# Sigmoid attention and two token-mixing layers on one core: pairs of token batches alternate in short runs of blocks, and attention takes its own order of work

## The chip, the cores and the metric

The kernel runs on one core of a Trainium2 chip. The metric is device time in microseconds (us) of the whole program. TensorE (PE) multiplies, VectorE (DVE), ScalarE (ACT) and GpSimd (POOL) work on the tiles in on-chip memory, and SyncE (SP) issues most DMA transfers. Each of these engines takes its instructions strictly in the order in which they were written.

## The reference, cut to what matters

```python
def _attn_ref(q, k, v):                       # q, k, v: (4, 12, 448, 64), float32
    scale = 1.0 / np.sqrt(q.shape[-1])
    scores = scale * np.matmul(q, k.transpose(0, 1, 3, 2)) - np.log(q.shape[2])
    return np.matmul(1.0 / (1.0 + np.exp(-scores)), v)
def _moe_ref(x, w_in, w_out):                 # x: (1792, 768), 2048 hidden columns
    h = x @ w_in
    return (h - np.tanh(h)) @ w_out
def _moe2_ref(x, w_gate, w_val, w_out):       # 1536 hidden columns
    gate = 1.0 / (1.0 + np.exp(-(x @ w_gate)))
    return (gate * (x @ w_val)) @ w_out
def reference(**kwargs):
    ...
    x = attn_out.transpose(0, 2, 1, 3).reshape(B * S, H * D)
    x = _moe_ref(x=x, **moe_kwargs)
    return _moe2_ref(x=x, **moe2_kwargs)
```

All is float32. The kernel holds each float32 operand as a high and a low part (fp32r) and makes one product of it out of three matmuls.

## The kernel before

**Attention** comes first: 24 pairs of heads, written by the loop at the end of the program. For a pair, `scores` (L1561 to L1597) multiplies keys and queries: PE fills the banks `sl` (L1573) and `sa` (L1588), and ACT takes the sigmoid out of them into `al` (L1577) and `at` (L1592, three a pair). `split` (L1525) is DVE's part: it divides keys and queries of the next pair into `sp` (seven instructions, L1538 to L1547), from which PE makes `sa`. `values` (L1616) multiplies the pair before with its values, and ACT copies the result into `x` (L1632). When the last pair of heads of a batch is done, `x` of that batch goes to DRAM as `xs` (L1634, 1,344 KB).

**The two layers** are worked through in 28 blocks of hidden columns for a pair of the four token batches. A block's hidden part is seven products of quarter tiles (`product`, L1996, 63 matmuls for each hidden matrix), over the terms a11, s1, s2, a12, s3, s4, a22 of x, some of them sums of quarters of x. `prepare` (L1415) makes these terms: the sums at L1435, the high part on ACT at L1443, the low parts on DVE or POOL at L1457. The projection of a block (`plain`, L1687, 72 matmuls; or `wide_fillers`, L1809, 63 matmuls) is worked into the hidden part of the block after it; the last one is `last_projections` (L1873). A block of layer 1 has 135 matmuls with a plain projection, one of layer 2 198, or 189 with a wide one.

**The passes.** The blocks run in four passes: layer 1 for the first pair of batches (8 blocks), layer 1 for the second (8), layer 2 for the first (6), layer 2 for the second (6). In the first pass of a layer the weights come from the inputs as raw words of 64 bits (`raw_task`, L1015, tiles `st`) and are decoded (`decode`, L1030): the absolute value on ACT (L1048), a clamp on DVE or POOL (L1054), and three more steps on DVE (L1061, L1067, L1073). The decoded words `mw` or `ms` are divided into high and low parts (`divide_for`, L1158: high on ACT L1186, low on DVE or POOL L1195, sums of quarters L1226, L1239), and the halves are stored in DRAM (L1206). In the second pass of the layer `bring` (L1261) loads the halves back (L1282) and nothing is decoded. Seven weights of layer 2 are decoded ahead, in the second pass of layer 1, and kept in DRAM as words (`MID`).

**The order** is written out by hand under `manual_schedule`. A planner in the program writes it: work other than matmuls is a `Task` (L860) with a due time and a list of operations, each with a planned cost on one or two engines, and `spend` (L932) lets the tasks onto the engines beside a stretch of matmuls, by due time. The times at which blocks and passes begin, the offsets of the due times and the choice of engines come from a table of numbers, `TUNE`. In the attention `tick` gives tasks half a pair's time, twice a pair:

```python
scores(p)
tick()
split(p + 1)
if p:
    load_v(p + 2)
    values(p - 1)
tick()
```

Names in the rows: `pa`, `pb`, `pc`, `pe` are PSUM banks of the hidden part, `pq` those of the projection, `sg` what the activation is taken of, `gg` its result divided again, `y` the sum over the blocks (L1673).

## Time and profile before

| | us |
|---|---|
| median of 3 runs | 1116.19 |
| the runs | 1116.50, 1116.19, 1112.31 |
| the profiled execution, its own time | 1112.16 |
| its span | 1110.4 |

| engine | busy in the span |
|---|---|
| PE (matmuls) | 1055.8 us, 95% |
| DVE | 872.5 us, 79% |
| ACT | 631.4 us, 57% |
| POOL | 286.6 us, 26% |

The rows further down come from the profiled execution, so sums are made against its 1112.16 us, of which 1.76 lie outside the span. PE is the engine with the most work; the time that it isn't at work at full pace can be read as losses: in a stretch with n matmuls of the layers, the stretch's length minus n times the length of one in an undisturbed stretch. The granted clock of PE is given for each window as a share of full speed.

### The profile page before, as it was taken

How to read it: one execution, taken by the hardware profiler on the slowest of the kernel's cores; microseconds unless marked ns; L12 is line 12 of the kernel's file. 1: busy time of each engine (PE TensorE's matmuls, PEld its weight loads, DVE VectorE, ACT ScalarE, POOL GpSimd, SP SyncE). 2: the span in 40 equal slices, each digit the busy share in tenths (PEclk: the TensorE clock that was granted, in tenths of full speed). 3: DMA queues.
4: the chain of work that ended last, by engine and by line, in shares of the span. 5: the costliest groups of instructions: out<-in, count | busy, mean ns of one | idle time of the engine just before them, and what ended most of it. 6: DMA issues, size and time to landing. Idle time of an engine off the chain costs nothing.

```text
span 1110.4 us, 16236 instructions
## 1 busy us (share of the span) xinstructions
PE 1055.8 (95%) x5895; PEld 943.3 (85%) x5895; DVE 872.5 (79%) x1432; ACT 631.4 (57%) x1038; POOL 286.6 (26%) x269
## 2 busy tenths in 40 slices
...
GB/s 214 235 287 214 266 117 341 181 182 176 208 185 183 216 213 213 213 199 228 213 214 99 185 341 214 199 203 296 219 320 218 272 206 138 165 182 189 173 9 102
...
## 3 DMA queue, kind: packets, MB, share of 16 engines
...
q10 hardware_dynamic: 160, 0.23, 0.1%
...
## 4 chain that ended last, share of the span: by engine, by line
PE 73%; DVE 12%; ACT 6%; DMA 3%; issue 3%; SPq 2%; POOL 1%; ACTq 0%; POOLq 0%; DVEq 0%
PE pq L1724 24%; PE pa L1996 11%; PE pb L1996 11%; PE pc L1996 11%; PE pe L1996 6%; PE pv L1626 3%; PE pq_c L1785 1%; DVE y L1673 1%; SPq L1504 1%; PE sa L1588 1%; PE pq_a L1785 1%; PE pq_b L1785 1%; DVE mw L1067 1%; PE sl L1573 1%; DVE mw L1073 1%
## 5 line engine op out<-in xcount | busy, mean ns | idle before, releaser
L1724 PE MATMUL pq<-gg,w 128*128 128x448 f32 x1656 | 357.9, 366 | 15.4 <-ACT y L1733 10.0
L1724 PEld LDWEIGHTS pq<-gg,w 128*128 128x128 f32 x1656 | 312.6, 189 | 41.5 <-ACT y L1733 11.5
L1996 PE MATMUL pa<-a,w_b 128*128 128x448 f32 x720 | 159.1, 365 | 4.7 <-DVE sg L2059 4.7
L1996 PEld LDWEIGHTS pa<-a,w_b 128*128 128x128 f32 x720 | 135.9, 189 | 14.9 <-DVE sg L2059 5.4
L1673 DVE TENSOR_TENSOR y<-pq,y 128x448 f32<-128x448 f32 x171 | 105.3, 619 | 27.5 <-PE pq L1724 26.8
L1195 POOL TENSOR_TENSOR w<-mw,w 128x384 fp32r<-128x384 f32 x29 | 33.8, 1170 | 215.8 <-ACT w L1186 160.5
L1996 PE MATMUL pb<-s,w_t 128*128 128x448 f32 x360 | 79.2, 363 | 2.6 <-ACT pb L2015 1.5
L1996 PE MATMUL pe<-s,w_t 128*128 128x448 f32 x360 | 79.3, 364 | 1.5 <-DVE sg L2059 1.1
L1996 PE MATMUL pb<-s,w_b 128*128 128x448 f32 x360 | 79.4, 364 | 1.0 <-DVE s L1457 1.0
L1996 PE MATMUL pc<-a,w_t 128*128 128x448 f32 x360 | 79.2, 363 | 1.0 <-DVE a L1457 0.6
L1996 PE MATMUL pc<-s,w_t 128*128 128x448 f32 x360 | 78.5, 362 | 0.0
L1996 PEld LDWEIGHTS pb<-s,w_t 128*128 128x128 f32 x360 | 67.1, 187 | 8.7 <-ACT pb L2015 2.3
L1996 PEld LDWEIGHTS pe<-s,w_t 128*128 128x128 f32 x360 | 67.9, 189 | 6.9 <-DVE sg L2059 1.5
L1996 PEld LDWEIGHTS pb<-s,w_b 128*128 128x128 f32 x360 | 68.2, 189 | 6.0 <-DVE s L1457 1.4
L1996 PEld LDWEIGHTS pc<-a,w_t 128*128 128x128 f32 x360 | 67.4, 187 | 6.5 <-DVE a L1457 1.3
L1996 PEld LDWEIGHTS pc<-s,w_t 128*128 128x128 f32 x360 | 67.5, 187 | 4.5
L1592 ACT ACTIVATE at<-sa,bias_s 128x896 f32<-128x896 f32 x72 | 67.1, 1008 | 5.4 <-PE sa L1588 5.4
L1626 PE MATMUL pv<-at,vt 128*64 128x224 f32 x576 | 63.5, 373 | 0.0
L1195 POOL TENSOR_TENSOR w_b<-mw,w_b 128x384 fp32r<-128x384 f32 x18 | 21.7, 1208 | 152.0 <-ACT w_b L1186 120.5
L1195 DVE TENSOR_TENSOR w_t<-mw,w_t 128x384 fp32r<-128x384 f32 x84 | 50.2, 633 | 11.6 <-ACT w_t L1186 11.3
L1626 PEld LDWEIGHTS pv<-at,vt 128*64 128x64 f32 x576 | 41.2, 143 | 20.9 <-issue 8.3
L1186 ACT ACTIVATE w_t<-mw 128x768 fp32r<-128x768 f32 x50 | 41.3, 841 | 29.3 <-DVE mw L1226 17.6
...
## 6 DMA issues: line engine op xcount, KB each, us to landing
...
```

Of the source, the lines that this page charges most:

```text
L1067: nc.vector.scalar_tensor_tensor(out=mine(), in0=t_[0][0][:, :, 1], scalar=-0x40000000, in1=mine(), op0=ALU.bitwise_and, op1=ALU.bitwise_or,)
L1073: nc.vector.scalar_tensor_tensor(out=mine(), in0=t_[0][0][:, :, 0], scalar=29, in1=mine(), op0=ALU.logical_shift_right, op1=ALU.bitwise_or,)
L1186: nc.scalar.activation(out=w0, in_=src, func=AF.Copy)
L1195: eng.tensor_tensor(out=w1, in0=quarter(m, qs[i]), in1=w0.bitcast(F32), op=ALU.subtract)
L1504: by.dma_start(out=t[r], in_=src[p, r, j])
L1573: nc.tensor.matmul(pl[h * KL:(h + 1) * KL, j, :SH], kt[r, KR:], qt[r, h * SH:(h + 1) * SH], start=True, stop=True,)
L1592: nc.scalar.activation(out=at[:, :, c], in_=pa[:, :, :S], func=AF.Sigmoid, bias=bias_s, scale=qk_scale,)
L1626: nc.tensor.matmul(po[j * D:(j + 1) * D, h, :SH], vt[:, j, c], at[:, j, c, h * SH:(h + 1) * SH], start=False, stop=(c == NCH - 2),)
L1673: nc.vector.tensor_tensor(out=at[:, d], in0=po, in1=at[:, d], op=ALU.add)
L1724: nc.tensor.matmul(po[:, :S], wk[use, j][:, a, d], gt[t][:, c, j], start=i == 0 and not seeded, stop=i == 5, skip_group_check=seeded,)
L1785: nc.tensor.matmul(o, w[:, a, h * KH + d], move[x](b), start=fresh and i == 0, stop=i == 2, skip_group_check=not fresh,)
L1996: nc.tensor.matmul(bank[term], w[:, i, half * KH + c], t[:, j, c], start=fresh and at == 0, stop=at == 3 * KH - 1, skip_group_check=not fresh,
```

## The change

The pairs of batches now alternate every 4 blocks in layer 1 and every 3 in layer 2 (`ORDER`): blocks 0 to 3 first pair, 4 to 11 second pair, 12 to 15 first pair; in layer 2 blocks 16 to 18 second pair, 19 to 24 first, 25 to 27 second. So blocks 0 to 3, 8 to 11, 16 to 18 and 22 to 24 decode their weights, and the others bring halves back. When a pair returns (block 12, block 25), the terms of x that were made for it the first time are loaded from DRAM (`again`), where `save` has put them: 14 transfers of 1,376 KB out and 14 back. Weights are decoded ahead and kept as words in three stretches in which halves are brought back: 1, 3 and 3 of them. The wide projections are those of blocks 25 to 27; before they were those of 22 to 25 and 27. The program has 18 matmuls more by this.

In the attention the loop gives tasks a whole pair's time once, after `scores` and `split`; the absolute value and the high parts may be taken by DVE there; the first conversions of x come in three pieces of 448 columns; raw words are asked for by the planned time of their first use; and `x` of batches 2 and 3 is stored after block 0. The clamp no longer goes to POOL. In the last projection three additions go to POOL by way of a copy. The count of misfits (a check at the change of layers) is a task, with its verdict two blocks later. `TUNE` has 1,145 entries instead of 711; its rows are left out here.

```diff
-TUNE = {'ahead': 117.79,
+TUNE = {'ahead': 88.65,
...
-    FIRST = [0, NF[0], 2 * NF[0], 2 * NF[0] + NF[1]]
-    NK = 2 * (NF[0] + NF[1])
-    PASS = [p for p in range(4) for _ in range(NF[p // 2])]
-    F_OF = [k - FIRST[PASS[k]] for k in range(NK)]
-    N1 = FIRST[2]
-    LAST = [len(PARTS[p // 2]) - 1 for p in PASS]
-    WIDE = TUNE.get("wide", [*range(FIRST[1], FIRST[2]), *range(FIRST[3], NK)])
+    ORDER = TUNE.get("order", (
+        (0, 0, 0, 4), (0, 1, 0, 4), (0, 1, 4, 8), (0, 0, 4, 8),
+        (1, 1, 0, 3), (1, 0, 0, 3), (1, 0, 3, 6), (1, 1, 3, 6),
+    ))
+    BLOCKS = [(l, p, f, n) for n, (l, p, f0, f1) in enumerate(ORDER) for f in range(f0, f1)]
+    NK = len(BLOCKS)
+    LAYER, PAIR, F_OF, SEG = ([b[i] for b in BLOCKS] for i in range(4))
+    DEC = [
+        not any(BLOCKS[j][0] == l and BLOCKS[j][2] == f for j in range(k))
+        for k, (l, p, f, n) in enumerate(BLOCKS)
+    ]
+    XS = [0]
+    for k_ in range(1, NK):
+        XS.append(XS[-1] + (BLOCKS[k_][:2] != BLOCKS[k_ - 1][:2]))
+    NSET = XS[-1] + 1
+    START = [XS.index(n) for n in range(NSET)]
+    STOPS = [*(n - 1 for n in START[1:]), NK - 1]
+    SET_OF = [(LAYER[n], PAIR[n]) for n in START]
+    SEG_AT = [SEG.index(n) for n in range(len(ORDER))] + [NK]
+    N1 = LAYER.index(1)
+    LAST = [len(PARTS[l]) - 1 for l in LAYER]
+    WIDE = TUNE.get("wide", range(START[-1], NK))
...
+        def plan(self):
+
+            n = len(self.ops)
+            d = [1e9] * n
+            for i in reversed(range(n)):
+                if self.by[i] is not None:
+                    d[i] = min(d[i], self.due + self.by[i])
+                if i < n - 1:
+                    d[i] = min(d[i], d[i + 1])
+                kinds, _, after, _, _ = self.ops[i]
+                before = d[i] - RF * min(kinds.values()) - RC
+                for j in after:
+                    d[j] = min(d[j], before)
+            self.dues = d
+            self.due = d[0]
...
-        def a():
+        def a(e="a"):
             t_.append(raw_t[key])
             t = t_[0][0]
+            if e == "v":
+                x = t[:, :, 1].bitcast(F32)
+                nc.vector.scalar_tensor_tensor(
+                    out=mine().bitcast(F32), in0=x, scalar=-1.0, in1=x, op0=ALU.mult, op1=ALU.max
+                )
+                return
...
-        def clamp(eng):
+        def clamp():
             m_ = mine()
-            eng.tensor_scalar(
+            nc.vector.tensor_scalar(
...
-        t = task.add(dict(a=0.78), a, (), gate)
-        t = task.add(dict(v=0.52, g=TUNE.get("pc", 1.9)), clamp, [t], lock=True)
+        t = task.add(dict(a=0.78, v=0.93) if now[0] < 0 else dict(a=0.78), a, (), gate, False)
+        t = task.add(dict(v=0.52), clamp, [t], lock=True)
...
-            for h in range(2):
-                raw_task(layer, part, 2 * f + h, due - TUNE.get("raw", 14.0) + 4.0 * h)
+        raws = [raw_task(layer, part, 2 * f + h, 0.0) for h in range(2)] if direct else ()
...
+        for raw, first in zip(raws, firsts if direct else ()):
+            raw.due = task.dues[first] - TUNE.get("raw", 5.0) + TUNE.get(raw.name, 0.0)
...
+            cost = dict(a=0.41, v=0.3) if small else dict(a=0.75, v=0.5)
+            if now[0] >= 0:
+                del cost["v"]
+            h = task.add(cost, high, after, gate, False)
...
-    ][:TUNE.get("early", 4)]
-    MID = [wid_of(u) for u in uses if PASS[u[0]] == 2][:TUNE.get("mid", 8)]
+        wid_of(u) for u in uses if SEG[u[0]] == 0 and u not in FIRST_USES
+    ][:TUNE.get("early", 2)]
+    MID = {}
+    for n_ in range(2, len(ORDER)):
+        if DEC[SEG_AT[n_]]:
+            a_, b_ = T[SEG_AT[n_ - 1]], T[SEG_AT[n_]]
+            mids = [wid_of(u) for u in uses if SEG[u[0]] == n_][:TUNE.get(f"mid{n_}", 4)]
+            for i, w in enumerate(mids):
+                MID[w] = a_ + (b_ - a_) * (i + 1) / (len(mids) + 0.5)
...
-        side = 0
+        side = early_side() if now[0] < 0 else 0
...
-        direct = PASS[k] % 2 == 0 and wid not in EARLY and wid not in MID
+        direct = DEC[k] and wid not in EARLY and wid not in MID
...
+            pieces = KH if p == 0 else 1
...
+        if SET_OF[p] in SET_OF[p + 1:]:
+            for term in TERMS:
+                save(p, term, conv[term])
+
+    def save(p, term, task):
+
+        keep = saves[p, term] = Task(
+            f"v{term}_{p}", T[START[p]] + 30.0 + 8.0 * TERMS.index(term), [task]
+        )
+
+        def f():
+            xk[p, term] = keep_p.tile([128, 2, KH, S], F32, tag=f"xk{term}{p}", name=f"xk{term}{p}_")
+            nc.sync.dma_start(out=xk[p, term], in_=xo[p, term].bitcast(F32))
+            xk_at[p, term] = keep.end[-1] + 1.0
+
+        keep.add(dict(s=1376.0), f, (), lambda: None if now[0] < 20.0 else BEGIN)
+
+    def again(p, first, due, pitch):
+        def one(term, due):
+            task = x_task[p, term] = Task(f"x{term}_{p}", due)
+
+            def gate():
+                free, got = x_free.get((p, term)), xk_at.get((first, term))
+                return None if free is None or got is None else max(free, got)
+
+            def load():
+                xo[p, term] = x_tile(PLACE[p][term], f"{term}_{p}")
+                nc.sync.dma_start(out=xo[p, term].bitcast(F32), in_=xk[first, term])
+
+            task.add(dict(s=1376.0), load, (), gate)
+
+        for i, term in enumerate(TERMS):
+            one(term, due + pitch * i)
...
-        if hp == KD - 1:
+        if hp == KD - 1 and b < 2:
...
+        copies = acc["temps"][:, KH:]
+        added = {}
+
         def p5(d, place):
             mm("p5", "e", d, place)
             then()
             evict(0, d, "e", d)
-            evict(0, KH + d, "e", d)
+            t = must("a", 0.465, lambda: nc.scalar.activation(
+                out=copies[:, d], in_=bank_of("e", d), func=AF.Copy
+            ))
+            held(place, t)
+            at = out_tile(k, 0)[:, KH + d]
+            added[d] = must("g", 1.07, lambda: nc.gpsimd.tensor_tensor(
+                out=at, in0=copies[:, d], in1=at, op=ALU.add
+            ), t)
...
-        lead = -TUNE.get("att", 14.0) / 1.0
-
-        def tick():
-            for e, cost in TUNE.get("base", dict(a=2.0, v=1.5, g=1.15, d=1.5)).items():
+
+        def pair_time():
+            for e, cost in TUNE.get("base", dict(v=2.7, g=2.6, d=3.0, s=3.0)).items():
                 busy[e] = max(busy[e], now[0]) + cost
-            spend(2.75, TUNE.get("tv", 0.4), TUNE.get("ta", 0.7))
-
+            busy["a"] = max(busy["a"], now[0] + TUNE.get("ra", 4.4))
+            spend(5.5, TUNE.get("tv", 0.6), TUNE.get("ta", 0.5))
+
+        gap = TUNE.get("gap", 11.0)
         for p in range(NP - 1):
-            if p == 1:
-                gap = TUNE.get("gap", 11.0)
+            if p == TUNE.get("p0", 2):
                 for i, job in enumerate(first):
                     create(job, BEGIN + 16.0 + gap * (i + 1))
             if p == NP // 2 + 1:
+                src_at[0] = now[0] + 6.0
                 prepare(0, TUNE.get("x0", -40.0), 6.0)
             scores(p)
-            tick()
             split(p + 1)
+            pair_time()
             if p:
                 load_v(p + 2)
                 values(p - 1)
-            tick()
...
-            if k == TUNE.get("x1", 3):
-                prepare(1, T[FIRST[1]] - 6.0)
-            if k == FIRST[1] + TUNE.get("x2", 1):
-                prepare(2, T[FIRST[2]] - 6.0)
-            if k == FIRST[2] + TUNE.get("x3", 1):
-                prepare(3, T[FIRST[3]] - 6.0)
-            if k:
-                create_until(T[k] + AHEAD)
-            if k == FIRST[3]:
+            for n in range(1, NSET):
+                reload_ = SET_OF[n] in SET_OF[:n]
+                if k == START[n] - TUNE.get(f"x{n}", 1 if reload_ else 2 if LAYER[START[n]] else 3):
+                    prepare(n, T[START[n]] - 6.0)
+            create_until(T[k] + AHEAD)
+            if k == START[-1]:
+                progress(raw_done, "the last raw words")
                 w_ring.free.append(NW)
             block(k, fillers)
             if k == 0:
-                create_until(T[1] + AHEAD)
+                for b in range(2, NB):
+                    nc.sync.dma_start(out=xs[b], in_=acc[0, b])
+                    src_at[1] = stored(now[0], 1376.0) + 1.0
             if k == N1:
+                misfits = count_misfits()
+            if k == N1 + 2:
+                misfits.finish()
                 verdict()
```

What this does to the order of the instructions is shown at three places.

On ACT in the attention, from the sigmoids of pair 1 to the copy of pair 1's values (`al1`, `at2`, `al2` are sigmoids of pairs 1 and 2, `x0` the result of batch 0, `mw0_0` the first decoded weight, `st00_0` its raw words). Before:

```order
L1592 ACTIVATE at1_218<-sa1_2_236,bias_s_91 128x2x448
L1577 ACTIVATE al1_219<-sl1_244,bias_s_91 128x448
L1632 ACTIVATE x0_87<-pv0_273 128x448
L1048 ACTIVATE mw0_0_291<-st00_0_250 128x768
L1592 ACTIVATE at2_293<-sa2_0_295,bias_s_91 128x2x448
L1592 ACTIVATE at2_293<-sa2_1_303,bias_s_91 128x2x448
L1592 ACTIVATE at2_293<-sa2_2_311,bias_s_91 128x2x448
```

and now:

```order
L2161 ACTIVATE at1_218<-sa1_2_236,bias_s_91 128x2x448
L2146 ACTIVATE al1_219<-sl1_244,bias_s_91 128x448
L2201 ACTIVATE x0_87<-pv0_273 128x448
L2161 ACTIVATE at2_291<-sa2_0_293,bias_s_91 128x2x448
L2161 ACTIVATE at2_291<-sa2_1_301,bias_s_91 128x2x448
L2161 ACTIVATE at2_291<-sa2_2_309,bias_s_91 128x2x448
L2146 ACTIVATE al2_292<-sl2_317,bias_s_91 128x448
L2201 ACTIVATE x0_87<-pv1_342 128x448
```

The absolute value (L1048) stood between the copy of x and the sigmoids of pair 2; it is gone from ACT's row there.

On DVE in the attention, between two splits (`sp2`, `sp3`, and now `sp4`, `sp5`). Before:

```order
L1546 CAST sp2_254<-qt2_131 128x448
L1547 TENSOR_TENSOR sp2_254<-qt2_131,sp2_254 128x448
L1054 TENSOR_SCALAR mw0_0_291<-mw0_0_291 128x768
L1061 TENSOR_SCALAR mw0_0_291<-mw0_0_291 128x768
L1538 CAST sp3_327<-kt3_167 128x3x112
L1538 CAST sp3_327<-kt3_167 128x3x16
```

and now:

```order
L2115 CAST sp4_392<-qt4_213 128x448
L2116 TENSOR_TENSOR sp4_392<-qt4_213,sp4_392 128x448
L1526 SCALAR_TENSOR_TENSOR mw0_0_405<-st00_0_263 128x768
L1536 TENSOR_SCALAR mw0_0_405<-mw0_0_405 128x768
L1543 TENSOR_SCALAR mw0_0_405<-mw0_0_405 128x768
L1549 SCALAR_TENSOR_TENSOR mw0_0_405<-st00_0_263,mw0_0_405 128x768
L2107 CAST sp5_466<-kt5_257 128x3x112
L2107 CAST sp5_466<-kt5_257 128x3x16
```

DVE now takes the absolute value itself (L1526), from the raw words, and three more steps of the same decoding between the splits of pairs 4 and 5.

On SP at the change to block 25 (`w25_0` and so on are halves brought back for it, `kept` words, `a11_5`, `s1_5` and so on the terms of x of the last set, `xk...` where they were saved). Before:

```order
L1282 DMA w24_1_b22_8726<-half1_1_2_b22_6581 128x768
L1282 DMA w25_0_b1_8744<-half1_0_3_b1_6718 128x1536
L1282 DMA w25_0_t14_8799<-half1_0_3_t14_6826 128x1536
L1282 DMA w25_0_t32_8875<-half1_0_3_t32_6869 128x1536
L1282 DMA w25_0_b22_8877<-half1_0_3_b22_6756 128x768
L1282 DMA w25_1_b1_8995<-half1_1_3_b1_7026 128x1536
L1282 DMA w25_1_t14_8997<-half1_1_3_t14_7143 128x1536
L1282 DMA w25_1_t32_9027<-half1_1_3_t32_7162 128x1536
L1282 DMA w25_1_b22_9029<-half1_1_3_b22_7031 128x768
L1118 DMA mw26_2_9031<-kept1_2_4_7542 128x1536
```

and now:

```order
L1783 DMA w25_0_b1_8758<-half1_0_3_b1_7726 128x1536
L1783 DMA w25_0_t14_8803<-half1_0_3_t14_7805 128x1536
L1608 DMA kept1_2_5_8808<-mw24_2_8649 128x1536
L2034 DMA a11_5_8833<-xka113__5662 128x2688
L2034 DMA s1_5_8843<-xks13__5709 128x2688
L2034 DMA s2_5_8863<-xks23__5743 128x2688
L1783 DMA w25_0_t32_8882<-half1_0_3_t32_7881 128x1536
L1783 DMA w25_0_b22_8884<-half1_0_3_b22_7758 128x768
L2034 DMA a12_5_8886<-xka123__5975 128x2688
L2034 DMA s3_5_8920<-xks33__5847 128x2688
L2034 DMA s4_5_8933<-xks43__5998 128x2688
L2034 DMA a22_5_8950<-xka223__5906 128x2688
```

The halves of the block's first hidden matrix are followed by the seven loads of terms of x, with the second half of those halves between them.

DVE's instructions by block (from a block's first matmul to the next block's) as the order has them:

| blocks | 1 | 2 | 3 | 4 | 5 | 6 | 7 | 8 | 9 | 10 | 11 | 12 | 13 | 14 | 15 |
|---|---|---|---|---|---|---|---|---|---|---|---|---|---|---|---|
| before | 44 | 32 | 52 | 41 | 42 | 37 | 47 | 36 | 33 | 31 | 33 | 35 | 36 | 36 | 48 |
| now | 44 | 44 | 37 | 31 | 29 | 24 | 39 | 41 | 43 | 33 | 35 | 29 | 34 | 36 | 49 |

Over the whole program DVE's row goes from 2,943 to 2,870 instructions, ACT's from 1,620 to 1,611, POOL's from 276 to 317 and SP's from 724 to 752; a second path of the program, which does not run here, is counted in them.

## Rows read from the trace of the kernel before

**Rows 1.** The windows: length, busy time (instructions), PE's clock share, DMA share, GB/s:

```profile
core 0: us, PE busy (x) PEld busy (x) DVE busy (x) ACT busy (x) POOL busy (x), PEclk, DMA share, GB/s
8.26:158.54 150.28, 132.88 (x1338) 92.72 (x1334) 103.70 (x203) 108.20 (x139) 67.35 (x100) 0.97 0.78 237
158.54:1102.94 944.40, 916.30 (x4529) 847.27 (x4525) 764.42 (x1216) 519.66 (x895) 212.16 (x153) 0.99 0.55 201
```

**Rows 2.** The page's first line: the span:

```profile
span 1110.4 us, 16236 instructions
```

**Rows 3.** The windows of single blocks: 2 and 18, undisturbed:

```profile
206.75:233.75 27.00, 27.00 (x137) 25.31 (x136) 24.82 (x39) 20.81 (x38) 6.23 (x5) 1.00 0.51 190
697.68:737.28 39.60, 39.60 (x200) 37.13 (x199) 37.00 (x57) 20.16 (x31) 6.09 (x6) 1.00 0.65 239
```

**Rows 4.** The windows: blocks 1 to 7, and of them 5 and 7:

```profile
177.59:392.24 214.65, 197.54 (x944) 180.58 (x945) 194.57 (x291) 145.65 (x264) 70.41 (x53) 0.97 0.55 200
296.60:330.68 34.08, 31.16 (x134) 28.15 (x135) 29.50 (x43) 19.67 (x37) 11.44 (x8) 0.88 0.44 151
358.10:392.24 34.14, 29.70 (x137) 26.33 (x136) 30.59 (x43) 23.75 (x42) 14.62 (x12) 0.95 0.56 209
```

**Rows 5.** The windows of blocks 1, 15 and 20:

```profile
177.59:206.75 29.16, 27.42 (x134) 25.04 (x135) 25.77 (x43) 19.48 (x37) 11.53 (x8) 1.00 0.68 257
583.90:616.23 32.33, 28.65 (x137) 26.39 (x136) 28.27 (x44) 21.57 (x37) 12.24 (x9) 0.95 0.34 127
776.88:818.82 41.94, 40.48 (x200) 36.77 (x199) 40.64 (x66) 25.32 (x39) 7.00 (x5) 1.00 0.73 272
```

**Rows 6.** The windows of attention pairs 2, 13 and 19:

```profile
14.39:28.51 14.12, 8.33 (x62) 5.37 (x58) 4.95 (x10) 4.65 (x6) 2.21 (x4) 0.76 0.78 229
86.83:97.76 10.93, 7.52 (x62) 4.86 (x58) 3.02 (x8) 5.18 (x8) 2.32 (x5) 0.84 0.88 279
130.37:135.84 5.47, 5.47 (x62) 3.92 (x58) 3.11 (x9) 4.69 (x6) 2.24 (x4) 1.00 0.67 217
```

**Rows 7.** PE's waits over the span: us in total, times, longest:

```profile
PE sl L1573 <- ACT at L1592: 12.3, 9, 5.8
PE pq L1724 <- ACT y L1733: 10.0, 4, 3.7
PE pa L1996 <- DVE sg L2059: 4.7, 2, 4.2
PE sa L1588 <- DVE sp L1546: 4.0, 3, 2.0
```

**Rows 8.** The timeline of pairs 2 and 13: start, busy, engine, operation [idle before]:

```profile
20.67 0.89 ACT L1048 ACTIVATE mw<-st 128x768 f32<-128x768 f32 x1 [5.37 <-DMA st<-in_w_in_dram]
22.51 0.63 PE L1573 MATMUL sl<-qt,kt 64*64 64x224 f32 x1 [5.79 <-ACT at L1592]
...
90.15 0.89 ACT L1048 ACTIVATE ms<-st 128x768 f32<-128x768 f32 x1 [2.41 <-DMA st<-in_w_out_dram]
```

**Rows 9.** The chain of waits between 80 and 100 us: start, us, what:

```profile
87.77 8.07 DMA xs<-x
```

**Rows 10.** Groups by line and shape: line, operation xcount | busy, mean ns:

```profile
L1673 DVE TENSOR_TENSOR y<-pq,y 128x448 f32<-128x448 f32 x171 | 105.3, 619 | 27.5 <-PE pq L1724 26.8
L1073 DVE SCALAR_TENSOR_TENSOR mw<-st,mw 128x768 int32<-128x768 int32 x48 | 50.3, 1050 | 0.8
L1067 DVE SCALAR_TENSOR_TENSOR mw<-st,mw 128x768 int32<-128x768 int32 x48 | 47.9, 997 | 0.6
```

**Rows 11.** The timeline from 99 to 106 us, DVE and POOL:

```profile
99.43 3.57 DVE L1073 SCALAR_TENSOR_TENSOR ms<-st,ms 128x768 int32<-128x768 int32 x1
...
105.49 0.95 DVE L1073 SCALAR_TENSOR_TENSOR ms<-st,ms 128x768 int32<-128x768 int32 x1
...
99.94 2.24 POOL L1457 TENSOR_TENSOR a<-x,a 128x448 fp32r<-128x448 f32 x2
```

**Rows 12.** The window with the most DMA traffic among those read:

```profile
760.00:780.00 20.00, 20.00 (x102) 18.75 (x101) 18.46 (x32) 12.31 (x19) 3.10 (x3) 1.00 0.97 370
```

1299 lines of the change are left out of this document (768 added, 531 removed), and 791 rows, old and new, of the table TUNE.

## Prediction

> **What bounds the kernel now.** I read the windows by stage first. The stretch of the 28 blocks [rows 1] is 944.4 us long and holds 4,525 weight loads, one for each matmul (a few matmul records are missing or doubled, so I count the loads). An undisturbed layer-1 block takes 27.00 us and has 135 matmuls by the program, an undisturbed layer-2 block 39.60 us and 198 [rows 3]: 0.200 us a matmul in both. 4,525 x 0.200 = 905.0, so the blocks lose 39.4 us. In the attention [rows 1] an undisturbed pair takes 5.47 us [rows 6]; 23 pairs at that pace are 125.8 of 150.28 us, so 24.5 are lost. With 8.26 us ahead of it and 7.46 us behind the last block (span [rows 2] less the window's end) the span is 8.3 + 125.8 + 24.5 + 905.0 + 39.4 + 7.5 = 1110.4. Only the 63.9 us of loss can move, up or down; PE's own work hardly changes.
>
> Then the windows of the blocks, for where the loss sits. Blocks 1 to 7 take 214.65 us instead of 7 x 27.00, a loss of 25.7 [rows 4]; block 15 loses 5.3 [rows 5]. That is 31.0 of 39.4. The reader is to see DVE there: 28 to 31 us busy in blocks 5, 7 and 15, more than the 27.00 that PE needs, against 24.82 in the undisturbed one [rows 3 to 5]. Block 20 loses 2.3 with DVE at 40.64 of 39.6 us [rows 5]. PE's waits say the same from the other side: `pq` waits for ACT's `y`, `pa` for DVE's `sg` [rows 7], both ends of chains through DVE.
>
> In the attention the largest wait is PE's for the sigmoids, 12.3 us [rows 7]. The timeline shows what held them: ACT's next instruction was the absolute value of a raw weight, which waited 5.37 us for its transfer; the sigmoids stood behind it, and PE idled 5.79 us. It comes again as 2.41 us at 90.15 [rows 8], with the x store of 8.07 us in the chain just ahead [rows 9]. Pairs 2 and 13 with these waits took 14.12 and 10.93 us, and show a granted clock of 0.76 and 0.84 [rows 6]: after such a stop part of the pair runs at the 1.2 GHz level, so a stop costs more than its length.
>
> **The change part by part.** *The alternation* spreads decoding. The order gives the DVE instructions of each block (table in the change). A DVE instruction in blocks 1 to 7 took 194.57 / 291 = 0.669 us [rows 4], so a block of 27.00 us holds 40. Before, blocks 1, 3, 4, 5, 7 and 15 have 41 to 52: loads of 29.4, 34.8, 27.4, 28.1, 31.4 and 32.1, together 21.2 us over 27. They and their neighbours lose 31.0, so 1.46 us for each microsecond over. Now blocks 1, 2, 8, 9 and 15 have 44, 44, 41, 43 and 49: 29.4, 29.4, 27.4, 28.8 and 32.8, together 12.8 over, times 1.46 = **18.7 us**. Bounds: nothing, as in the blocks of rows 3, and 7.1 a block, the worst of before [rows 4], 35.5. The relief is in blocks 3 to 7, where the order has 160 instructions instead of 219, and it is partly paid for in 2, 8 and 9.
>
> *The other block losses* are 39.4 - 31.0 = 8.4 us before (changes of pass and layer, block 12, block 20, the last). Clamps leave POOL, and layer 2's decoding is in two shorter runs; both changes of layer and pass stay. I take **4**, between 0 and 12.
>
> *Eighteen more matmuls* (fewer wide projections): 18 x 0.200 = **3.6 us**, all on PE's path.
>
> *Saving and reloading x* adds 38.5 MB. At the blocks' mean of 201 GB/s and a DMA share of 0.55 [rows 1] there is room on average; what counts is the three crowded places. The stretch before block 25 must bring seven terms (9.6 MB) and, between them on SP's queue, some 3.9 MB of halves and words. At the 370 GB/s of the busiest window [rows 12] that is 37 us. The first place for a term is free early in block 24, and the last term is wanted some 6 us into block 25: 45.6 us. So it hides, with 9 us to spare; block 12 has the same with less around it. The stores in block 1 (two of x, seven terms, 12.4 MB, 33 us at that rate) have nobody waiting but the raw loads queued behind them on SP. I take 0 for these, and the far end is a rival below. What the cover is: PE's work of blocks 24, 11 and 1.
>
> *Attention.* In the order ACT has no absolute value ahead of sigmoids in the first pairs, and later ones stand behind a pair's last sigmoid: a late raw word then has most of a pair to arrive. The 12.3 us of waits and the slow clock behind them go. What is next is DVE: the wait moves to its queue, where the absolute values now stand, with the splits of later pairs behind them, and `sa` on PE waits for the splits (4.0 us before [rows 7]). Over pairs 4 to 22 DVE has 185 instructions instead of 173. At the stage's 103.70 / 203 = 0.511 us [rows 1] and with the 12 more at 0.997 (two-input operation of the same size, L1067 [rows 10]) this is 88.4 + 12.0 = 100.4 us over 19 pairs, 5.28 us a pair under PE's 5.47. It fits, barely. I take a loss of **6 us** (the 4.0 for splits stays, 2 for the start) instead of 24.5; bounds 2 and 14 (14 if only the two stops of rows 8 and their slow clock go). ACT is spared 0.89 us for each absolute value moved [rows 8].
>
> *POOL* gets 49 more low parts, products and additions, loses 8 clamps. An operation on POOL can stretch one on DVE: L1073 took 3.57 us beside two POOL operations of 2.24 us, against a mean of 1.050 [rows 10, 11]. That is up to 1.26 us for each POOL operation, where DVE is spared about 0.62 to 0.75 (L1673's 0.619 for the same width [rows 10]). So what DVE gains from a move lies between +0.7 and -0.6 us; I take nothing, and the DVE counts above already leave these operations out. The Trainium skill (Perfetto Trace Analysis, section Optimizing Scalar/DVE Operations) says that GpSimd and DVE share a read port, "so offloading operations between those two might not help". The trace agrees in this one pair of rows; by the rule the moved work would be no relief, which is the third rival.
>
> *Sum.* 8.3 + 125.8 + 6 + 905.0 + 3.6 + 18.7 + 4 + 7.5 = 1078.9 us of span; with the 1.76 outside it, 1080.7 against the profiled execution's 1112.16. The runs shown have a median 4.0 above that execution and a lowest run 0.15 above it; I add half, 2: **1083 us**, 3% below the median before.
>
> **The rivals.** *DVE's queue is relieved for good*: decoding slips into slack, tight blocks lose about 1 us each instead of 3.7 (18.7 becomes 5), attention loses 3: 1083 - 13.7 - 3 = 1066. For it: the total over blocks 1 to 7 falls from 295 to 248 instructions, 165.9 us of 189. Against it: blocks below 40 instructions lost too where a chain ended late.
>
> *DVE becomes the attention's bound*: 5.28 us a pair stretched by 10% (L1073's mean of 1.050 [rows 10] is that much over the 0.95 of one without company [rows 11]) is 5.81, 0.34 over for 19 pairs, 6 us; and raw words late by 5.37 and 2.41 [rows 8] now hold DVE and with it the splits: 8. Together 1083 + 14 = 1097. For it: the margin of 4%. Against: raw loads are asked for by the planned use.
>
> *What POOL takes is no relief*: some two POOL operations more in each of the five tight blocks, at 1.26 less 0.3 for the share that misses a DVE operation, 1.9 us a block, times 1.46 and 5: 14, also 1097. For it: rows 11. Against: in the undisturbed blocks POOL is busy 6 us beside a DVE without loss [rows 3].
>
> *Slower: transfers don't keep up at the changes of pair.* If the large transfers run as the x store did, 1.376 MB in 8.07 us or 170 GB/s [rows 9], the 13.6 MB before block 25 take 80 us of 45.6, 34 late; block 12 is 10 late; in block 1 the raw words behind the stores come some 25 late. 1083 + 69 = 1152; with half of it 1117, so it is slower than before once the rate lies under some 230 GB/s, and costs nothing above 13.6 / 45.6 = 298. Against: 370 GB/s at a share of 0.97 in a window where stores and loads are mixed [rows 12]; the x store was issued in a stretch that was crowded with others at 279 GB/s [rows 6].
>
> *Nothing gained*: the attention keeps its 24.5 (late words hold DVE as they held ACT) and the blocks 31: 1083 + 18 + 12 = 1113.
>
> **How the numbers follow.** Forecast (1073 to 1090) 0.47; relieved for good 0.13; DVE bounds the attention 0.13; POOL no relief 0.08; nothing gained 0.07; transfers late 0.12. The predicted time is the first's, 1083. For 8 in 10 the range leaves out the late transfers, the unchanged case and a little of the quickest: 1063 to 1107, which also takes in each unknown's bounds alone (attention 2 to 14, tight blocks from nothing to 35.5). About 0.5%, 6 us, is what a measurement of this kernel can tell from no change. Faster by more: 0.47 + 0.13 + 0.13 + 0.08 = 0.81; within: 0.07; slower: 0.12.
>
> **What would show it.** Right: PE's wait for `at` falls from 12.3 to under 2 us and pairs 2 and 13 take under 6; blocks 3 to 7 take 27 to 28 us each, blocks 1, 2, 9 and 15 28 to 32; the window of blocks 24 and 25 shows no wait of PE for `a11` to `a22` and over 300 GB/s. Wrong: pairs of 6 us with PE waiting for `sp` (DVE in the attention); PE waits for DMA at blocks 12 or 25 (transfers); blocks 3 to 7 still over 29 us though DVE has less to do (then the load was not what bound them).

## The result

The changed kernel takes 1078.76 us in the median of 4 runs (1073.35 to 1083.64), the kernel before on the same chip 1114.25: a ratio of 0.9683, 95% interval 0.9620 to 0.9747. The forecast was 1083, with 1063 to 1107 around it. The profiled execution took 1073.35 us with a span of 1071.4, 39.0 less than the span of before [rows 2]; it is one of the two quicker runs (1073 and 1075, the others 1082 and 1084).

The windows of the changed kernel, columns as in [rows 1] here and below: the attention, all blocks, the blocks of layer 1 and of layer 2, then attention pairs 2, 13 and 17, and blocks 3 and 15:

```profile
8.44:136.45 128.01, 126.58 (x1338) 90.27 (x1334) 106.10 (x219) 99.64 (x133) 57.07 (x92) 1.00 0.93 270
136.45:1064.01 927.56, 912.25 (x4547) 846.76 (x4543) 712.55 (x1127) 517.53 (x892) 251.37 (x202) 1.00 0.66 248
136.45:571.00 434.55, 425.04 (x2123) 393.44 (x2120) 349.51 (x555) 295.25 (x540) 125.99 (x103) 1.00 0.65 249
571.00:1064.01 493.01, 487.21 (x2426) 453.32 (x2424) 363.04 (x574) 222.27 (x353) 125.38 (x99) 1.00 0.66 247
14.57:20.04 5.47, 5.47 (x62) 3.93 (x58) 4.21 (x12) 3.87 (x5) 2.21 (x4) 1.00 0.74 202
74.84:80.32 5.48, 5.48 (x62) 3.93 (x58) 3.91 (x9) 3.87 (x5) 2.21 (x4) 1.00 1.10 308
96.75:103.58 6.83, 5.52 (x62) 3.93 (x58) 6.66 (x12) 5.96 (x10) 3.41 (x5) 1.00 0.74 184
212.69:243.83 31.14, 27.55 (x137) 25.15 (x136) 29.94 (x48) 20.52 (x33) 17.12 (x12) 1.00 0.57 216
543.85:571.00 27.15, 27.15 (x137) 25.23 (x136) 24.25 (x39) 22.93 (x39) 13.03 (x11) 1.00 0.84 328
```

Of the 39.0 us, 22.3 come from the attention (150.28 to 128.01 [rows 1]) and 16.8 from the blocks (944.40 to 927.56); the two ends lose 0.1. Against 23 pairs of 5.47 us the attention's loss falls from 24.5 to 2.2 us: all but two pairs take 5.47 to 5.49, the first of the window 6.13 and pair 17 6.83. At 0.200 us a matmul the loss of the blocks falls from 39.4 to 927.56 - 4,543 x 0.200 = 19.0. In layer 1 it is 434.55 - 2,120 x 0.200 = 10.6, and in layer 2 493.01 - 2,424 x 0.200 = 8.2. The kernel before has 33.7 and 5.5 there, by its two windows:

```profile
158.54:616.23 457.69, 433.15 (x2123) 397.33 (x2120) 389.51 (x597) 297.42 (x538) 125.39 (x87) 0.98 0.54 201
616.23:1102.94 486.71, 483.15 (x2408) 449.94 (x2406) 374.91 (x620) 222.23 (x357) 86.77 (x66) 1.00 0.55 202
```

PE's waits over the span of the changed kernel (us in total, times, longest), against [rows 7]:

```profile
PE pc L2588 <- DVE s L1966: 3.3, 1, 3.3
PE pq L2294 <- ACT y L2303: 2.5, 3, 1.0
PE pb L2588 <- DVE w_t L1689: 2.3, 1, 2.3
...
PE sl L2142 <- ACT at L2161: 1.3, 1, 1.3
```

The wait for the sigmoids went from 12.3 us to 1.3, and that for ACT's `y` from 10.0 to 2.5. The longest left is block 0's for the term s3 of x.

### The profile page after: what moved, and what is told of

Read it like the earlier page. It is cut to its first block, busy times and chain, and to the rows that moved or that the text cites. A ratio compares the mean times of both kernels' runs of the same rounds, so it can differ in the third digit from the quotient of the medians.

```text
span 1071.4 us, 16265 instructions
## 1 busy us (share of the span) xinstructions
PE 1045.2 (98%) x5913; PEld 940.3 (88%) x5913; DVE 823.0 (77%) x1359; ACT 620.7 (58%) x1029; POOL 315.7 (29%) x310
## 4 chain that ended last, share of the span: by engine, by line
PE 78%; DVE 14%; ACT 3%; DMA 2%; issue 2%; POOL 1%; SPq 0%; DVEq 0%; ACTq 0%; POOLq 0%
PE pq L2294 26%; PE pc L2588 11%; PE pa L2588 11%; PE pb L2588 11%; PE pe L2588 6%; PE pv L2195 5%; PE sa L2157 3%; DVE y L2241 2%; PE sl L2142 1%; DMA st<-in_w_out_dram 1%; DVE gg L2751 1%; DVE mw L1549 1%; DVE w_t L1689 1%; DVE s L1989 1%; PE pq_c L2355 1%
## 5 line engine op out<-in xcount | busy, mean ns | idle before, releaser
L2294 PE MATMUL pq<-gg,w 128*128 128x448 f32 x1800 | 384.1, 363 | 5.7 <-ACT y L2303 2.5
L2294 PEld LDWEIGHTS pq<-gg,w 128*128 128x128 f32 x1800 | 336.8, 187 | 32.2 <-ACT y L2303 3.6
L2241 DVE TENSOR_TENSOR y<-pq,y 128x448 f32<-128x448 f32 x175 | 107.5, 618 | 58.0 <-PE pq L2294 57.7
L1689 POOL TENSOR_TENSOR w<-mw,w 128x384 fp32r<-128x384 f32 x33 | 38.8, 1188 | 205.1 <-ACT w L1680 180.5
L2588 PE MATMUL pc<-s,w_t 128*128 128x448 f32 x360 | 80.7, 368 | 4.6 <-DVE s L1966 3.3
L2588 PEld LDWEIGHTS pc<-s,w_t 128*128 128x128 f32 x360 | 68.4, 190 | 10.4 <-issue 3.6
L1689 POOL TENSOR_TENSOR w_t<-mw,w_t 128x384 fp32r<-128x384 f32 x36 | 38.3, 1080 | 116.4 <-ACT w_t L1680 101.4
L2746 ACT ACTIVATE gg<-sg 128x896 fp32r<-128x896 f32 x50 | 47.4, 948 | 36.5 <-DVE sg L2615 24.7
L2751 POOL TENSOR_TENSOR gg<-sg,gg 128x448 fp32r<-128x448 f32 x31 | 41.8, 1363 | 90.0 <-ACT gg L2746 83.0
L2195 PE MATMUL pv<-at,vt 128*64 128x224 f32 x576 | 59.8, 357 | 0.0
L1689 POOL TENSOR_TENSOR w_b<-mw,w_b 128x384 fp32r<-128x384 f32 x22 | 25.9, 1193 | 114.0 <-ACT w_b L1680 105.6
```

The costliest lines, as they stand in the source:

```text
L1689: eng.tensor_tensor(out=w1, in0=quarter(m, qs[i]), in1=w0.bitcast(F32), op=ALU.subtract)
L2195: nc.tensor.matmul(po[j * D:(j + 1) * D, h, :SH], vt[:, j, c], at[:, j, c, h * SH:(h + 1) * SH], start=False, stop=(c == NCH - 2),)
L2241: nc.vector.tensor_tensor(out=at[:, d], in0=po, in1=at[:, d], op=ALU.add)
L2294: nc.tensor.matmul(po[:, :S], wk[use, j][:, a, d], gt[t][:, c, j], start=i == 0 and not seeded, stop=i == 5, skip_group_check=seeded,)
L2588: nc.tensor.matmul(bank[term], w[:, i, half * KH + c], t[:, j, c], start=fresh and at == 0, stop=at == 3 * KH - 1, skip_group_check=not fresh,
L2746: h = task.add(dict(a=0.86), lambda: nc.scalar.activation(out=gt_tile(t)[:, 0], in_=sg[t], func=AF.Copy), (), gate_)
```

## The experiments

The runs that have a ratio below were executed four times, the others once, and each has one profile. The changed kernel's own four runs lie 10 us apart, so a few us between single runs of the blocks say nothing.

**Attention: the place in the queue, or words that land late?** The first run changes only the loop in the kernel before, so that ACT's absolute value stands behind a pair's last sigmoid:

```diff
-        def tick():
-            for e, cost in TUNE.get("base", dict(a=2.0, v=1.5, g=1.15, d=1.5)).items():
+        def pair_time():
+            for e, cost in dict(v=2.7, g=2.6, d=3.0).items():
                 busy[e] = max(busy[e], now[0]) + cost
-            spend(2.75, TUNE.get("tv", 0.4), TUNE.get("ta", 0.7))
+            busy["a"] = max(busy["a"], now[0] + 4.4)
+            spend(5.5, 0.6, 0.5)
...
             scores(p)
-            tick()
             split(p + 1)
+            pair_time()
             if p:
                 load_v(p + 2)
                 values(p - 1)
-            tick()
```

> The kernel before with one thing changed: in the attention's loop a pair takes scores, split, one stretch of tasks, values, and ACT is reserved until a pair's last sigmoid, so that the absolute value of raw words stands behind it; blocks, passes and table stay. Theory (the place of the absolute value in ACT's queue made the attention's loss): the attention falls from 150.3 to 130-134 us, PE's wait for the sigmoids from 12.3 to under 3 us, pairs 2 and 13 to under 7 us; the blocks stay at 944 to 952 us; time 1094 to 1102. Rival (the raw words themselves are late, wherever the wait stands): attention still above 143, time above 1105. Rival (DVE then bounds the attention): pairs of 6 us, PE waiting for sp.

It took 1129.06 us, 1.0114 of the kernel before (1.0083 to 1.0145): longer by 1.1%, little but clear of noise, where 1094 to 1102 was expected. Its windows of attention, blocks, and blocks 1 to 7, and PE's wait in the attention:

```profile
8.68:146.29 137.61, 127.94 (x1338) 90.84 (x1334) 87.84 (x195) 105.69 (x136) 54.73 (x90) 0.99 0.83 246
146.29:1122.25 975.96, 930.78 (x4529) 855.62 (x4525) 771.54 (x1239) 523.63 (x898) 200.78 (x148) 0.98 0.53 197
174.44:407.15 232.71, 207.37 (x944) 186.89 (x945) 193.42 (x302) 147.21 (x268) 60.88 (x49) 0.93 0.52 192
```
```profile
PE sl L1573 <- ACT at L1592: 9.6, 4, 3.1
```

The attention gained 12.7 us, and its 137.6 lie between the 130 to 134 of the theory and the 143 of its rival; 9.6 us of waits for the sigmoids stay. The blocks lost 31.6 more. DVE did 195 instructions in the attention instead of 203 [rows 1] and 23 more in the blocks; in blocks 1 to 7 it has 302 in place of 291, the clock share falls to 0.93 and they take 18 us longer [rows 4]. DVE's busy time hardly moved (771.54 instead of 764.42 us in all blocks, 193.42 instead of 194.57 in blocks 1 to 7), so the amount of DVE's work is not what cost 31.6 us. That the table, made for the old loop, no longer fits is a rival that no run tests.

The second run changes one number in the kernel before: in the attention the planner counts raw words as landed 3 us later, as the changed kernel does.

```diff
-            raw_at[layer, part, u] = task.end[-1]
+            raw_at[layer, part, u] = task.end[-1] + (3.0 if now[0] < 0 else 0.0)
```

> The kernel before with that one number alone: raw words count as landed 3 us later in the attention. Theory (late words): attention falls from 150.3 to 132-140 us, PE's wait for the sigmoids under 5 us; since some of the decoding is put off, blocks 0 to 8 lose 5 to 30 us more, as in the run with the loop alone. Rival (the place in ACT's queue): attention stays above 146, as the absolute value still stands ahead of sigmoids.

Span 1117.5 us, time 1119.31 beside 1114.85:

```profile
8.47:142.68 134.21, 127.49 (x1338) 90.30 (x1334) 96.91 (x198) 106.97 (x138) 64.13 (x98) 1.00 0.88 265
142.68:1110.09 967.41, 924.44 (x4529) 851.70 (x4525) 763.91 (x1231) 520.84 (x896) 197.77 (x145) 0.98 0.54 197
```

The attention gained 16.1 us with the absolute value still ahead of sigmoids, and the wait for the sigmoids fell to 5.1 us. ACT's own waits for raw words in the attention go with it: 8.8 us in the kernel before, 13.4 in the first run, none here. So the lateness of the words weighs at least as much as the place. The blocks lost more than was gained (23.0), again without more work on DVE (763.91 us busy).

The third takes that margin away from the changed kernel:

```diff
-            raw_at[layer, part, u] = task.end[-1] + (TUNE.get("rl", 3.0) if now[0] < 0 else 0.0)
+            raw_at[layer, part, u] = task.end[-1] + (0.0 if now[0] < 0 else 0.0)
```

> The changed kernel without the 3 us that the planner adds to the landing of raw words in the attention; the first absolute value then stands one pair earlier on DVE, ahead of the split of pair 4. Theory (raw words that land later than planned made the attention's loss, and the added time cures it): DVE waits for words with splits behind it, attention 133 to 145 us instead of 128, PE waits for sp. Rival (the loop's order cures it): attention under 130.

Span 1087.7 us. The attention's window, and the timelines of DVE and PE (start, busy, engine, operation, in brackets the idle time before and what ended it):

```profile
8.39:146.22 137.83, 130.08 (x1338) 91.61 (x1334) 103.02 (x222) 99.86 (x134) 50.84 (x87) 0.98 0.85 251
```
```profile
24.35 0.96 DVE L1526 SCALAR_TENSOR_TENSOR mw<-st 128x768 f32<-128x768 f32 x1 [8.23 <-DMA st<-in_w_in_dram]
...
29.02 3.25 PE L2157 MATMUL sa<-sp 64*128 64x448 f32 x18 [3.22 <-DVE sp L2115]
```

This is the new wait that the prediction named: the absolute value now waits on DVE, the split of pair 4 stands behind it, and PE waits 3.22 us for `sp`. The attention lost 9.8 us; its 137.8 lie in the 133 to 145 of the theory. The rest of the change thus brings the attention 12.5 us without the margin, and 22.3 with it.

The fourth puts the old loop back into the changed kernel, with the absolute value on ACT alone; the fifth keeps the loop and only puts the absolute value back on ACT. Both keep the margin:

```diff
-        t = task.add(dict(a=0.78, v=0.93) if now[0] < 0 else dict(a=0.78), a, (), gate, False)
+        t = task.add(dict(a=0.78), a, (), gate, False)
...
+        def tick():
+            for e, cost in dict(a=2.0, v=1.5, g=1.15, d=1.5).items():
+                busy[e] = max(busy[e], now[0]) + cost
+            spend(2.75, 0.4, 0.7)
...
             scores(p)
+            tick()
             split(p + 1)
-            pair_time()
             if p:
                 load_v(p + 2)
                 values(p - 1)
+            tick()
```

> The changed kernel with the attention's loop of before (tasks in two halves of a pair, split between them) and the absolute value on ACT alone; all else stays. Theory: absolute values stand ahead of sigmoids again at several pairs, attention 138 to 150 us instead of 128, PE waits for the sigmoids for over 5 us; span 1083 to 1095. Rival (the raw loads' new due times or the moved x stores gave the gain): attention stays under 132 us.

> The changed kernel with the absolute value on ACT alone in the attention; it stands behind a pair's last sigmoid there, ahead of the copy of the values. Theory (the place decides, not the engine): attention 128 to 132 us, span within 4 us of 1071.4. Rival (DVE had to take it): attention above 135 us with PE's wait for the sigmoids back above 5 us.

 (Only the first pair of lines of the diff.)

Old loop, span 1083.0, then ACT alone, span 1087.7 (attention and blocks, and in the second its block 3):

```profile
8.39:139.76 131.37, 127.55 (x1338) 90.31 (x1334) 101.57 (x208) 102.93 (x139) 58.29 (x94) 1.00 0.86 255
139.76:1073.87 934.11, 915.13 (x4547) 848.43 (x4543) 719.02 (x1135) 516.76 (x892) 249.63 (x198) 0.99 0.65 247
```
```profile
8.54:137.38 128.84, 126.77 (x1338) 90.17 (x1334) 93.41 (x209) 102.28 (x137) 51.13 (x87) 1.00 0.89 259
214.53:256.81 42.28, 33.72 (x137) 30.01 (x136) 32.67 (x47) 21.63 (x36) 13.54 (x10) 0.84 0.45 168
```

My theory fell for the old loop: 131.4 us, not 138 to 150. ACT waited for no raw word there, and words that have landed hold nobody, wherever the instruction stands; with the margin the place is worth about 3 us. The rival of that run, the raw loads' new due times and the moved x stores, isn't parted from the margin by it; the margin's own runs are the second and third. And the engine matters little in the attention (128.8). The span of the fifth run still missed the 4 us that I allowed, by 12: the loss sits in the blocks, 11 us of it in block 3 (42.28 instead of 31.14), a block to which I come back below.

**Blocks: is it the alternation?** First the changed kernel with the four passes:

```diff
-        (0, 0, 0, 4), (0, 1, 0, 4), (0, 1, 4, 8), (0, 0, 4, 8),
-        (1, 1, 0, 3), (1, 0, 0, 3), (1, 0, 3, 6), (1, 1, 3, 6),
+        (0, 0, 0, 4), (0, 0, 4, 8), (0, 1, 0, 4), (0, 1, 4, 8),
+        (1, 0, 0, 3), (1, 0, 3, 6), (1, 1, 0, 3), (1, 1, 3, 6),
```

> The changed kernel with the blocks of before in four passes (no alternation, so no saving and reloading of x); its code, table and attention stay, and the table was made for the other order. Theory (alternation spreads DVE's work): attention 128 us as in the changed kernel; the order has 308 instead of 254 DVE instructions in blocks 1 to 7, and 70 to 78 in blocks 16 and 18; blocks lose 40 to 60 us instead of 19, time 1095 to 1115. Rival (the blocks gained from other parts of the edit, clamps on DVE and due times by operation): within 8 us of the changed kernel, below 1085.

It took 1183.83 us (1.0616, 1.0591 to 1.0641) where 1095 to 1115 was expected; attention 127.65 and blocks 1037.61 us. That is far worse than either kernel, and no fair measure: the table's numbers are bound to block numbers of the other order. So both orders were run with an empty table:

```diff
-TUNE = {'ahead': 88.65,
...
+TUNE = {'mid2': 1, 'mid4': 3, 'mid6': 3}
```

The other has the four passes as above and `{'mid4': 7, 'mid5': 0, 'wide': [25, 26, 27]}`, with the seven weights decoded ahead spread over blocks 8 to 15.

> The changed kernel with an empty table, but for 1, 3 and 3 weights decoded ahead: every due time and choice by the planner's defaults. Theory (alternation itself is the gain in the blocks): blocks lose at least 15 us less than those of the next kernel, 30 to 60 us in all. Rival (the table is the gain): within 8 us of the next kernel's blocks, both losing over 60 us.

> The same with the four passes of before, 7 weights decoded ahead over the second pass, and wide projections in blocks 25 to 27 as in the kernel above; no saving and reloading of x. Theory: blocks lose 60 to 100 us. Rival: as the kernel above, within 8 us. By the DVE instructions over a block's time the order has 73 us here and 67 above, worth 9 us at 1.46.

Alternating, span 1153.8; passes, span 1157.9 (attention and blocks of each):

```profile
8.83:135.49 126.66, 126.61 (x1338) 90.13 (x1334) 104.51 (x216) 96.87 (x128) 53.22 (x89) 1.00 0.84 247
135.49:1146.57 1011.08, 946.04 (x4547) 861.29 (x4543) 700.66 (x1112) 569.39 (x984) 247.88 (x206) 0.96 0.59 223
```
```profile
8.67:135.21 126.54, 126.37 (x1336) 90.27 (x1334) 104.63 (x216) 96.77 (x128) 54.28 (x89) 1.00 0.85 248
135.21:1149.94 1014.73, 946.39 (x4547) 862.25 (x4543) 699.54 (x1102) 569.23 (x984) 262.15 (x216) 0.96 0.50 182
```

Same matmuls, and 3.7 us apart in the blocks, less than two executions of the changed kernel can differ by: the rival holds here. Without its table the alternation has no more room than the passes; it moves the losses (102 us against 106). Blocks 4 to 9 lose 57 us in the passes and 26 in the alternation, with 187 and 138 us of work on DVE, and the alternation loses the rest elsewhere. So DVE's work is spread as planned, and the blocks gain nothing clear by it. The table is worth 1011.08 - 927.56 = 83.5 us to the changed kernel's blocks. The attention needs no table: 126.5 to 126.7 us, below the changed kernel's 128.0. Whether the alternation with its table could be reached by the passes with a table as good stays open; the passes' own table stands in the kernel before, at 39.4 us of loss, but with the older planner. Nor were the clamps on DVE and the due times by operation run by themselves.

**POOL's share.** All low parts, products and sums go to DVE (costs for POOL out of reach); only the three additions of the last projection stay:

```diff
-    EITHER = dict(v=0.485, g=0.93)
+    EITHER = dict(v=0.485, g=9999.0)
...
-                task.add(dict(v=0.55, g=1.07), low, [h])
+                task.add(dict(v=0.55, g=9999.0), low, [h])
...
```

> The changed kernel with all low parts, products and sums on DVE and none on POOL, but for the three additions at the end; POOL only issues its transfers. The order then has 46 us more of DVE work over a block's time in layer 1 and 21 in layer 2. Theory (POOL's share is a relief of DVE): blocks lose 50 to 120 us instead of 19, span 1100 to 1170. Rival (the two engines share a port, so POOL's work costs DVE as much as it spares): span within 10 us of 1071.4, and DVE's operations of one kind take less time each than in the changed kernel.

Span 1121.7 us. Its blocks, then groups on DVE (line, operation, xcount | busy us, mean ns) of it and of the changed kernel:

```profile
137.62:1111.93 974.31, 927.74 (x4547) 855.88 (x4543) 761.44 (x1328) 518.77 (x891) 3.75 (x3) 0.98 0.63 236
```
```profile
L2751 DVE TENSOR_TENSOR gg<-sg,gg 128x448 fp32r<-128x448 f32 x100 | 58.4, 618 | 10.9 <-ACT gg L2746 10.6
...
L1689 DVE TENSOR_TENSOR w_t<-mw,w_t 128x384 fp32r<-128x384 f32 x92 | 47.6, 551 | 12.1 <-ACT w_t L1680 12.0
```
```profile
L2751 DVE TENSOR_TENSOR gg<-sg,gg 128x448 fp32r<-128x448 f32 x69 | 46.8, 706 | 9.9 <-ACT gg L2746 9.7
...
L1689 DVE TENSOR_TENSOR w_t<-mw,w_t 128x384 fp32r<-128x384 f32 x56 | 35.4, 666 | 4.7 <-ACT w_t L1680 4.7
```

Theory and rival each hold a part. DVE took on 201 instructions in the blocks (1,127 to 1,328) and was busy only 48.9 us longer: 0.24 us for each, where one takes 0.55 to 0.62 without company. So more than half of what POOL takes over DVE pays back in stretched operations (`w_t` 551 to 666 ns). An operation with an input in a PSUM bank wasn't stretched: `y<-pq,y` took 619 ns without POOL's work beside it and 618 with it. The remaining 0.24 is real relief: without it the blocks lost 65.7 us instead of 19.0, a price that holds some table mismatch too. Between the two kernels POOL's share in the blocks grew from 153 operations [rows 1] to 202; at 0.24 us each that is an estimated 12 us of DVE time, which may be a part of the blocks' gain. No run tests it alone, and the two runs without a table have 206 and 216 and still lose over 100 us. The Trainium skill (SBUF — State Buffer, section SBUF: two separate sides) calls the port that both engines use an exclusive lock. The rows agree as far as they show the stretch; they add that moving work still paid.

**The reloads.** In the changed kernel each reload lands ahead of its use, closest for a12 at block 25. Issue on SP and time to landing, then PE's first use:

```profile
L2034 SPq DMA_DIRECT2D a<-xka__5975 x1: 437/437/437, 926.8 to 926.8; - x1
...
DMA to landing us min/median/max: 12.8/12.8/12.8
```
```profile
943.76 1.96 PE L2588 MATMUL pa<-a,w_b 128*128 128x448 f32 x9
```

926.8 + 12.8 = 939.6, so 4.2 us to spare (at block 12 the closest is 7.4). Two runs measure what that margin is worth:

```diff
                 nc.sync.dma_start(out=xo[p, term].bitcast(F32), in_=xk[first, term])
+                nc.sync.dma_start(out=xo[p, term].bitcast(F32), in_=xk[first, term])
```

> The changed kernel with each of the 14 reloads of x terms written twice to SP's queue, 19.3 MB more. In the changed kernel the stretch with the first reloads (block 11) runs at 413 GB/s and a full DMA share, that before block 25 at 311. Theory (transfers hide, with 9 us to spare before block 25): 9.6 MB more are 23 to 26 us; block 12 late by 10 to 25, block 25 by 8 to 20; span 1090 to 1115, with PE waiting for terms of x. Rival (transfers hide amply): span within 4 us of 1071.4. Rival (the chip moves them at 170 GB/s as the early x store): block 12 and 25 late by over 40 each.

and, with the copy going to DRAM instead of the same tile,

```diff
                 nc.sync.dma_start(out=xo[p, term].bitcast(F32), in_=xk[first, term])
+                again_ = keep_p.tile([128, 2, KH, S], F32, tag=f"xd{term}{p}", name=f"xd{term}{p}_")
+                nc.sync.dma_start(out=again_, in_=xk[first, term])
```

> The changed kernel with a copy of the same 1,376 KB from DRAM to DRAM issued behind each of the 14 reloads: the same extra bytes as when each reload is written twice, but nothing that the queue has to wait for. In the changed kernel's trace the reloads land 7.4 us or more ahead of their use at block 12 and 4.2 us or more at block 25. Theory (the margin is those microseconds, and the rate 311 to 413 GB/s): 9.6 MB more are 23 to 31 us; block 12 loses 8 to 20 us, block 25 10 to 25, most of it in PE's waits for terms of x or halves; span 1090 to 1115. Rival (the 78 us of the run with reloads written twice are the price of bytes): each block again loses over 30. Rival (the extra bytes find room): span within 4 us of 1071.4.

Blocks 12 and 25 of the first (span 1149.6) and SP's timeline in it, then the same blocks of the second (span 1107.5) with PE's waits from block 12 on:

```profile
470.42:530.96 60.54, 36.16 (x137) 31.46 (x136) 15.63 (x28) 20.10 (x38) 3.94 (x4) 0.75 0.85 329
976.17:1048.93 72.76, 47.17 (x200) 41.57 (x199) 15.79 (x24) 10.33 (x18) 12.02 (x12) 0.84 0.83 320
```
```profile
445.67 0.32 SPq L2034 DMA_DIRECT2D a<-xka__2147  x1
455.49 0.32 SPq L2035 DMA_DIRECT2D a<-xka__2147  x1
```
```profile
469.75:508.13 38.38, 30.98 (x137) 27.70 (x136) 15.54 (x28) 19.83 (x38) 3.98 (x4) 0.91 1.00 420
954.68:1008.05 53.37, 42.45 (x200) 37.87 (x199) 15.79 (x24) 10.31 (x18) 12.01 (x12) 0.94 1.01 405
```
```profile
PE pb L2590 <- DMA w_t<-half_t: 9.7, 2, 7.3
PE pc L2590 <- DMA a<-xka__2165: 4.7, 1, 4.7
```

The first run doesn't measure bytes, and its forecast missed (span 1090 to 1115): the second load into the same tile waited on SP until the first had landed, 9.8 us here and 8.2 to 10.4 over the 14, and all of the queue with it. It lost 33.5 us at block 12 and 33.2 at block 25. The second run is the clean one: 11.4 and 13.8 us at 405 to 420 GB/s, inside the 8 to 20 and 10 to 25 expected. Of PE's waits for transfers there, 9.7 us are for halves of weights queued behind the terms and 7.8 for the terms; most of the rest went to the lower clock after the waits (0.91 and 0.94).

**A try at a better version.** Block 0 waits 3.3 us for s3, whose place holds a decoded weight until late. Swapping the two places frees it one weight earlier:

```diff
-        return side_of[0] % 2 * 2
+        return (side_of[0] + 1) % 2 * 2
```

> The changed kernel with the two places for the first decoded weights taken in the other order, so that the place that the term s3 of x needs comes free one weight earlier; from block 4 on the order is the same. Theory (block 0 waits 3.3 us for s3, and 1.9 us more go to the lower clock after it, because its conversion starts late): block 0 loses under 0.5 instead of 2, its wait is gone, blocks 1 to 3 within 4 us of theirs; span 1064 to 1072, time against the kernel before 0.962 to 0.969. Rival (what is gained at s3 is lost at block 1's or 3's weights): span 1071 to 1080.

1080.61 us (1079.64 to 1081.23), ratio 0.9698 (0.9681 to 0.9714): not told from the changed kernel's 0.9683. Block 0's loss went from 2.0 to 1.1, not under 0.5, and block 3 took 37.32 us instead of 31.14. The span of 1078.4 is the rival's, but its cause isn't shown: the changed kernel's own order takes 37 us in block 3 in some executions, as follows.

**Block 3.** It took 37.66 us in the run with copies and 37.07 in the run with doubled loads, and up to there these two have the same instructions as the changed kernel. So of three profiled executions of one order, one took 31 us and two 37. The changed kernel first: DVE, POOL, PE, and a window behind its first wait of 2.3 us:

```profile
226.51 0.62 DVE L2751 TENSOR_TENSOR gg<-sg,gg 128x448 fp32r<-128x448 f32 x1
...
227.50 1.18 POOL L1989 TENSOR_TENSOR s<-x,s 128x448 fp32r<-128x448 f32 x1 [3.39 <-ACT s L1968]
...
238.57 3.88 PE L2294 MATMUL pq<-gg,w 128*128 128x448 f32 x18 [1.28 <-DVE y L2241]
```
```profile
221.00:224.00 3.00, 3.00 (x17) 2.81 (x16) 2.20 (x5) 0.89 (x3) 3.00 (x2) 1.00 1.01 305
```

and the kernel with copies: DVE, POOL, PE, the window behind the same wait, and its block 3; then block 3 of the run with doubled loads:

```profile
229.09 1.58 DVE L2753 TENSOR_TENSOR gg<-sg,gg 128x448 fp32r<-128x448 f32 x1
...
228.65 1.54 POOL L1989 TENSOR_TENSOR s<-x,s 128x448 fp32r<-128x448 f32 x1 [3.40 <-ACT s L1968]
...
244.03 2.23 PE L2296 MATMUL pq<-gg,w 128*128 128x448 f32 x5 [3.98 <-DVE y L2243]
```
```profile
222.00:225.00 3.00, 3.00 (x10) 2.69 (x9) 2.21 (x5) 1.04 (x3) 3.00 (x2) 0.51 1.05 317
213.84:251.50 37.66, 31.36 (x137) 28.34 (x136) 34.74 (x50) 22.07 (x36) 18.07 (x12) 0.86 0.48 181
```
```profile
214.56:251.63 37.07, 30.77 (x137) 27.84 (x136) 34.65 (x51) 22.09 (x36) 18.09 (x12) 0.91 0.49 187
```

PE had waited 2.3 us for a weight's low part in all three. In the changed kernel the granted clock stayed at its upper level after that (1.00); in the one with copies PE went on at 1.2 GHz for a while (0.51 in the window shown), which cost 1.6 us. DVE, waiting for banks from the slower PE, came to its product just after POOL had begun instead of just before, and both were stretched; PE then waited 4.0 us for `y` instead of 1.3, and lost 2.2 more at the lower clock after it. Together that is the 6.5 us between the two. The run with doubled loads shows the same: the wait of 2.3, the lower clock, 4.0 for `y`. Whether this block also makes the 8 us or so between the changed kernel's runs is not shown, since only one of them was profiled.

## Why the prediction was right, and where it was not

- *Sum.* Predicted span 1078.9, measured 1071.4 in the profiled run (1073.2, 1080.3 and 1081.6 in the others). The attention's loss was 2.2 us instead of 6, the blocks' 19.0 instead of 22.7; the rest of the sum stood (3.6 us for the matmuls, 126 for the pairs, 7.4 at the end). That the blocks came so near is luck: two terms were off by more, in opposite ways (tight blocks and other block losses, below).
- *Attention: effect right, cause half right.* The prediction put the wait down to ACT's order. The runs show that words landing later than planned make it, and that there are two remedies which overlap: moving the instruction behind the sigmoids gains 12.7 us, 3 us of margin alone 16.1, the whole change 22.3; with the margin in place the old order costs 3.4. The added 3 us stand in the change, and I gave them no term. The warning that the wait moves to DVE was right, as the run without margin shows.
- *DVE in the attention.* 219 instructions took 106.10 us of 128.01, so the rival in which DVE bounds a pair did not come about.
- *Tight blocks: mis-sized, and in the wrong places.* Predicted 18.7 for blocks 1, 2, 8, 9 and 15; measured 0.2, 1.1, 2.0, 0 and 0.2 there, 3.5 in all. Block 3 lost 4.1, where the table of counts showed 37 instructions and 48 ran. The step that failed is counting by the order: DVE runs ahead of or behind PE, so the block in which an instruction is written isn't that in which it runs. For block 15 the order has 49, and 39 ran. The rows of before could have told: block 2 has 32 in the order and 39 in [rows 3].
- *Other block losses: mis-sized too.* 4 was allowed, at most 12; measured some 15, of it 8.2 in layer 2 (5.5 before) and 7 in layer 1, mostly blocks 3 and 0. With 2.2 in the attention and 3.5 in the five blocks, two terms lie nearer to the first rival, relief for good (3 and 5), than to the forecast (6 and 18.7); its time of 1066 failed by this third term.
- *That the alternation spreads DVE's work* and so brings the gain is not shown. With empty tables it spread the work and the blocks were 3.7 us apart, which is no clear gain. The gain in layer 1 belongs to alternation, table and the other edits of the planner together, and the runs can't part them.
- *Signs.* Those of the attention came (PE's wait for `at` 1.3, pairs 2 and 13 at 5.47 and 5.48), and so did that of blocks 24 and 25 (no wait, 311 and 360 GB/s). That of the tight blocks failed: of blocks 1, 2, 9 and 15 only block 2 took 28 us, and block 3, forecast at 27 to 28, took 31.14.
- *Reloads.* Hidden, as forecast, but with 4.2 us to spare, not 9; the rate, 405 to 420 GB/s under load, was above the 370 I used [rows 12], while each transfer took 8.8 to 16.8 us to land. The slow rival's 170 GB/s never appeared.
- *POOL.* Taken as no gain and no loss; measured as 0.24 us of relief for each operation, an estimated 12 us of DVE time for the 49 that went there.
